# Planning the main slots one early slot sooner, and a pool of their own for the token tiles

## The chip, the core and the metric

The kernel runs on one core of a Trainium2 chip. The metric is the device time of one execution in microseconds. Before the change three runs had a median of 809.41 us (807.67 to 811.24).

## What is computed

A linear attention whose output goes through a mixture of experts with one expert per token. There are 8 batches, 8 heads, 576 positions per batch and head size 64, so 4608 tokens of width 512, and 8 experts with an inner width of 1024. All data are float32.

```python
proj = x @ w_phi                                   # x is q or k, 64 -> 128
proj = proj - max(abs(proj), axis=-1)              # the "differences"
phi  = concatenate([exp(proj), exp(-proj)])
num, den = phi(q) @ (phi(k).T @ v), phi(q) @ sum(phi(k))
x = num / (den + 1e-6)                             # heads side by side: 512 wide
logits = x @ w_gate                                # 8 experts
# the expert of a token: the best one, or that of the token before it (a second gate)
h   = maximum(x @ w1[e], 0)
out = softmax(logits)[e] * (h @ w2[e])
```

Which tokens go to which expert is known only at run time, after the attention. The kernel therefore plans on the chip: it writes lists of tokens per expert to DRAM, works out slots from the counts, reads the lists back and gathers the rows of x.

## The kernel before

**Attention.** `run` goes over 144 chunks of 128 tokens in pairs (`step`). For a pair it projects q and k (`proj`, L210), takes the largest absolute value `m` and subtracts it (L213, L215; the result `sb` holds the differences), takes exponentials for k (`kp`), turns q's differences and takes theirs (`qtr`, L230, L233; `qp`, eight buffers in the pool `feat`), adds up k's features with v (`kv`, L252) and multiplies q's features with that sum (`num`, L311, with results in `xo`, which SyncE writes to DRAM). The right side of the on-chip memory holds, from the outer edge inwards, the pools `front2` (inputs kq and v, 20,128 bytes per partition), `front3` (m, sb, kp, 28,768 bytes) and `feat` (32,768 bytes). On the left lie the constants, the early weights, `moe_xg` (raw weights and gathered tokens), `back2` and `small` (the list buffer `lr` among it).

**Gates.** After every quarter of the tokens `gate` finds each token's expert and its place in that expert's list, counts tokens per expert (`cnt`), and writes list entries by nine scatters of GpSimd (L554). The last gate runs while the first early slot is already being computed; `soon` is a list of eight functions called between the matmul groups of that slot's layer 1, and the last of them (`rest`) finishes the gate with its scatters.

**Slots.** A slot is a run of tokens of one expert. A unit is 128 tokens. There are three early slots of two units each (here called e0, e1, e2), planned during the attention from the gates of the first two and three quarters, and after them the main slots: 3 of four units, 7 of two units, and single and half units. For the main slots `plan_main` makes the plan. It is a generator that is advanced by `more`:

- The first call counts units per expert on TensorE (L637, twice), does some 75 small operations on VectorE (L639 to L785) and issues three list reads on GpSimd (L615; two for the halves, one for all other slots). These must follow all scatters.
- The second call turns the list on TensorE (L628) and copies token numbers and probabilities (`p_tokm`, `p_probm`, L629 and L630).

**A slot's work** (`slots`). `tokens` turns the gathered tokens on TensorE (L903) and splits each into a high and a low part (`xhi` by ScalarE L912, `xlo` by VectorE L913). `layer1` has four groups of 24 matmuls with results in one of two PSUM buffers, from which ScalarE makes `hh` (L952) and VectorE `hl` (L953). `layer2` has 24 matmuls per unit; VectorE scales the result into `y` (L1004) and GpSimd scatters it to the output (L1007). For the early slots layer 2 has one PSUM buffer (`psm4`), later there are two more (`psr`). Every matrix product is three matmuls of high and low parts (L917 to L919).

**Weights.** A slot needs eight tiles of weights, four for each layer. SyncE loads each as 512 KB into a raw buffer (`load`, L840), ScalarE casts it to `whi` (L850), VectorE makes `wlo` (L851). A slot's first load is preceded by reading its expert's number into a register (L827). There are 8 pairs of buffers for weights on the left from the start, 4 on the right from `open_main` on, and one more from `open_rest` on; raw buffers are 3 in `moe_xg` and, from `open_rest` on, 3 more in `moe_l1`, which lies where `back2` and `small` were. The main slots' loads come in program order behind all three early slots.

**Order.** Inside a block a scheduler orders each engine's instructions ahead of time, by their place in the program and by when it expects them to be ready. On the chip each engine then follows that order, each instruction waiting for what it needs. `here` and `issue_after` tie an instruction behind another on the same engine.

Where the calls of `more` stand before: `slots` is called for the early slots with `asides={1: more}` and `final=more`. So the first call stands behind layer 1 of e1 and before its layer 2; the second stands inside layer 1 of e2, behind its second group.

`open_main` opens the right weight pool and behind it one pool `moe_x2` with all of xhi, xlo, hh, hl, y and yl (38,912 bytes), in the place of `front3` and `feat`.

Of the kernel before, what the change touches and what calls it, by code (L numbers as in the profile page):

```python
# [7 lines left out]
F32R = mybir.dt.float32r  # L8
# [41 lines left out]
class Kernel:  # L50
# [9 lines left out]
    def run(self):  # L60
        nc, tc, A = self.nc, self.tc, self.A
        act, dve = self.act, self.dve
        with ExitStack() as root:
            self.const = self.mkpool(root, "const", 1, "left")
            dram = self.mkpool(root, "dram", 1, "left", DRAM)
            self.xs = dram.tile([NT + 1, DM], F32, name="xs")


            self.lst = dram.tile([E * NT + 128, PLACE], F32, name="lst")
            first = self.const.tile([128, 256], F32, name="first")  # L70
            self.sp.dma_start(first[:, 128:256], A["first"][:, 384:512])
            self.ident, self.w2 = first[:, 0:128], first[:, 128:256]
            self.cnt = self.const.tile([128, E], BF16, name="cnt")
            dve.memset(self.cnt, 0.0)

            warm = self.const.tile([128, E], BF16, name="warm")
            act.activation(warm, self.cnt, AF.Exp)

            self.wgi = self.const.tile([128, NHP, 2, 9], F32, name="wgi")
            self.pool.memset(self.wgi, 0.0)  # L80

            self.vs = [[self.const.tile([128, 2, D + 1], F32, name=f"vs{k}{b}") for b in (0, 1)] for k in (0, 1)]
            for x in self.vs:
                for t in x:
                    self.pool.memset(t, 0.0)

            self.moe_early = self.mkpool(root, "moe_e", WE, "left")
            self.mxg = self.mkpool(root, "moe_xg", 2, "left")
            back, front = ExitStack(), ExitStack()
            self.back2 = self.mkpool(back, "back2", 2, "left")  # L90
            self.small = self.mkpool(back, "small", 1, "left")

            self.pr = self.small.tile([128, 2, NC, PLACE], F32, name="pr")
            self.pool.memset(self.pr, 0.0)
            self.pskv = self.mkpool(back, "pskv", 1, "left", PSUM)
            self.psb = self.mkpool(back, "psb", 2, "left", PSUM)


            self.front2 = self.mkpool(front, "front2", 2, "right")
            self.front3 = self.mkpool(front, "front3", 3, "right")  # L100
            self.feat = self.mkpool(front, "feat", 8, "right")
            self.psf = self.mkpool(front, "psf", 2, "right", PSUM)
            self.wphases = [(self.moe_early, WE)]

            self.scattering = False
            self.tail, self.eslots, self.scattered = False, [], []
            self.g, self.ch, self.kvb, self.lg = {}, {}, {}, {}
            n = NBP * NHP * NC
            self.todo, self.turns, self.gates, self.background = [], [], [], []
            self.fetched = 0  # L110
            for gi in range(3):
                self.fetch_kqv(gi)
                if gi == 0:
                    self.sp.dma_start(first[:, 0:128], A["first"][:, 256:384])
                    self.consts()
            with tc.manual_schedule(engines={mybir.EngineType.PE}):
                for p in range(n // 2):
                    while self.fetched < n // 3 and self.fetched * 3 < 2 * p + 8:
                        self.fetch_kqv(self.fetched)
                    if FILL <= p < FILL + 4:  # L120
                        self.fill(p - FILL)
                    self.step(p, n)
            self.tail = True
            p = n // 2
            while p < n // 2 + KVLAG + 1 or self.todo or self.turns or self.gates:
                self.step(p, n)
                p += 1
            for x in self.background:
                for _ in x:
                    pass  # L130
            front.close()
            self.open_main(root)
            plan = self.plan_main()
            more = lambda: next(plan, None)
            go = self.advance

            def rest():
                for _ in self.last_gate:
                    pass
            no = lambda: None  # L140
            self.slots(self.eslots, {1: more}, more, soon=[no, self.fetched_last, go, no, go, no, go, rest])
            back.close()
            self.open_rest(root)
            self.moe()
# [503 lines left out]
    def plan_early(self, bp):  # L648
# [39 lines left out]
        if bp == 1:  # L688
            yield from self.early_chores(slots, got())
        else:  # L690

            g = got()
            for x in g:
                if not self.scattering:
                    break
                yield x

            def last():
                for _ in g:
                    pass  # L700
                for s in slots:
                    self.gather_x(s)

            def soon():
                with self.tc.high_priority():
                    last()
            self.fetched_last = soon
# [95 lines left out]

    def open_main(self, root):
        self.w_right = self.mkpool(root, "moe_wr", WR, "right")
        self.mx2 = self.mkpool(root, "moe_x2", 2, "right")
        self.psm4 = self.mkpool(root, "moe_ps1", 1, "right", PSUM)
        self.psl = self.mkpool(root, "moe_ps2", 2, "right", PSUM)
        self.wphases = [(self.moe_early, WE), (self.w_right, WR)]
# [80 lines left out]
    def tokens(self, s, g, late=False):  # L890

        pe, act, dve = self.pe, self.act, self.dve
        if "xg" not in s:
            self.gather_x(s)

        def step(k, u):
            if k == 0:
                s.setdefault("x", []).append([self.mx2.tile([128, 4, 256], F32R, name=n) for n in ("xhi", "xlo")])
            hi, lo = s["x"][g]
            t = self.turned()  # L900
            with self.here() if late else nullcontext():
                for d in range(4):
                    pe.transpose(t[:, d, :], s["xg"][u][:, d * 128:d * 128 + 128], self.ident)  # L903
            self.parts(s, hi, lo, slice(k * 128, k * 128 + 128), t)
        return [lambda k=k: step(k, sum(s["n"][:g]) + k) for k in range(s["n"][g])]
# [107 lines left out]
            else:  # L1013
                held.append(put)

    def slots(self, order, asides={}, final=None, held=None, soon=()):
        first = order[0]
        for g in range(len(first["n"])):
            for f in self.tokens(first, g):
                f()  # L1020
        self.held = len(first.get("w", ()))
        self.coming = list(order)
        for i, s in enumerate(order):
            while len(s.get("w", ())) < 8:
                self.spare()
            new = order[i + 1] if i + 1 < len(order) else None
            last = len(s["n"]) - 1
            for gi in range(last):
                self.layer1(s, gi, [])
            between = self.tokens(new, 0, bool(soon) and i == 0) if new else [lambda: None, final] if final else []  # L1030
            rest = self.layer1(s, last, between, () if i else soon)
            if i in asides:
                asides[i]()
            for f in between:
                f()
            for gi in range(last + 1):
                self.layer2(s, gi, rest, None if new else held)
            if new and len(new["n"]) == 2:
                for f in self.tokens(new, 1):
                    f()  # L1040
            s.clear()

    def guarded(self, slots, count, i, per):
        if i < len(slots):
            with self.tc.If(count > per * i):
                self.slots([slots[i]])
                self.guarded(slots, count, i + 1, per)
# [103 lines left out]
```

## Time and profile before

| what | value |
|---|---|
| median of 3 runs | 809.41 us |
| the profiled execution | 808.84 us |
| its span, first to last instruction | 807.1 us |
| mean granted clock of TensorE | 0.993 |
| DMA moved | 151.33 MB, mean 188 GB/s |
| weight loads `wraw` | 136 of 512 KB, median 5.0 to 6.0 us to landing |
| weight casts L850 on ScalarE | 136, 1048 ns each |
| weight splits L851 on VectorE | 128, 1222 ns each |
| gathers `xg` for the main slots | 32, median 6.7 us to landing |

Times in the profile are in microseconds from the first instruction. In a timeline a row gives the start, the duration, the engine, the line of the kernel, the operation, what it writes and reads, the number of merged instructions, and in brackets how long the engine had been idle and who released it. PE is TensorE, DVE VectorE, ACT ScalarE, POOL GpSimd, SP SyncE; a small q after the name stands for the engine's sequencer or DMA queue. In the table of waits stand the waiting engine with its tile and line, the awaited one, and the total, the number and the longest of these waits. Matmul durations overlap, so a long row of matmuls takes less time than their sum.

### The profile page before, as it was taken

How to read it: one execution, taken by the hardware profiler on the slowest of the kernel's cores; microseconds unless marked ns; L12 is line 12 of the kernel's file. 1: busy time of each engine (PE TensorE's matmuls, PEld its weight loads, DVE VectorE, ACT ScalarE, POOL GpSimd, SP SyncE). 2: the span in 40 equal slices, each digit the busy share in tenths (PEclk: the TensorE clock that was granted, in tenths of full speed). 3: DMA queues.
4: the chain of work that ended last, by engine and by line, in shares of the span. 5: the costliest groups of instructions: out<-in, count | busy, mean ns of one | idle time of the engine just before them, and what ended most of it. 6: DMA issues, size and time to landing. Idle time of an engine off the chain costs nothing.

```text
span 807.1 us, 23180 instructions
## 1 busy us (share of the span) xinstructions
PE 772.1 (96%) x9674; PEld 679.6 (84%) x9674; DVE 513.5 (64%) x940; ACT 401.1 (50%) x708; POOL 156.1 (19%) x165
## 2 busy tenths in 40 slices
PE   6899999999999998999799999999999999999993
PEld 5899989998898887987698997698988988589883
DVE  5687798789878886766653224643866823768621
ACT  4666666666587565351542123532745713657410
POOL 0000001200275241153411102201421311110100
PEclk9999999999999999999999999999999999999998
DMA  6754445444677714451952775832966769959300
GB/s 197 220 150 130 135 129 143 131 135 128 184 233 226 211 52 126 141 186 48 385 186 90 269 276 209 288 97 97 362 200 203 265 236 411 349 193 319 117 27 15
DMA packets 77231, 151.33 MB, mean 188 GB/s; under 512 B 8524, under 2 KB 50828, under 8 KB 77078
## 3 DMA queue, kind: packets, MB, share of 16 engines
q1 hardware_dynamic: 67424, 127.33, 47.9%
q0 software_dynamic: 7424, 20.08, 7.0%
q10 hardware_dynamic: 2272, 2.37, 0.9%
q8 instruction: 78, 1.28, 0.6%
q14 instruction: 33, 0.27, 0.1%
HBM read 128.21 MB, written 22.06 MB: 186 GB/s over the span
## 4 chain that ended last, share of the span: by engine, by line
PE 64%; issue 15%; DMA 8%; DVE 7%; POOL 2%; ACT 2%; SPq 1%; POOLq 0%; DVEq 0%; ACTq 0%
PE l L917 10%; PE l L918 10%; PE l L919 10%; PE kvp L252 8%; PE pj L210 8%; PE nm L311 8%; PE qt L230 4%; DMA out<-y,p_tokm 4%; DMA wraw<-in_w2h 2%; PE l L930 2%; POOL out L1007 1%; DVE m L213 1%; DVE sb L215 1%; PE nm L290 1%; PE tr L903 1%
## 5 line engine op out<-in xcount | busy, mean ns | idle before, releaser
L850 ACT CAST whi<-wraw 128x1024 fp32r<-128x1024 f32 x136 | 142.1, 1048 | 153.8 <-PE l L919 68.2
L851 DVE TENSOR_TENSOR wlo<-wraw,whi 128x1024 fp32r<-128x1024 f32 x128 | 156.0, 1222 | 77.4 <-ACT whi L850 76.4
L917 PE MATMUL l<-xhi,whi 128*128 128x256 f32 x512 | 146.9, 287 | 1.3 <-ACT xhi L912 1.3
L918 PE MATMUL l<-xlo,whi 128*128 128x256 f32 x512 | 144.6, 282 | 1.3 <-DVE xlo L913 1.3
L919 PE MATMUL l<-xhi,wlo 128*128 128x256 f32 x512 | 144.7, 283 | 0.0
L917 PE MATMUL l<-whi,hh 128*128 128x512 f32 x288 | 115.0, 399 | 5.5 <-DVE y L1004 5.4
L213 DVE TENSOR_REDUCE m<-pj 128x8 f32<-128x1024 f32 x72 | 87.8, 1219 | 44.7 <-PE pj L210 43.4
L919 PE MATMUL l<-whi,hl 128*128 128x512 f32 x288 | 114.0, 396 | 1.0 <-DVE hl L953 1.0
L918 PE MATMUL l<-wlo,hh 128*128 128x512 f32 x288 | 114.1, 396 | 0.0
L233 ACT ACTIVATE qp<-qt 128x512 f32<-128x512 f32 x144 | 84.6, 604 | 53.5 <-PE qt L230 53.1
L219 ACT ACTIVATE kp<-sb 128x512 f32<-128x512 f32 x144 | 82.8, 622 | 51.1 <-DVE sb L215 43.4
L917 PEld LDWEIGHTS l<-xhi,whi 128*128 128x128 f32 x512 | 97.0, 190 | 3.5 <-issue 2.2
L918 PEld LDWEIGHTS l<-xlo,whi 128*128 128x128 f32 x512 | 97.1, 190 | 1.8 <-DVE xlo L913 1.5
L919 PEld LDWEIGHTS l<-xhi,wlo 128*128 128x128 f32 x512 | 97.0, 190 | 0.1
L210 PE MATMUL pj<-first,kq 64*128 64x128 f32 x1152 | 86.4, 291 | 6.2 <-DMA kq<-in_kqT 6.2
L215 DVE TENSOR_TENSOR sb<-pj,m 128x1024 f32<-128x1024 f32 x72 | 88.1, 1224 | 4.1
L311 PE MATMUL nm<-kvs,qp 128*64 128x74 f32 x2304 | 86.3, 228 | 1.0 <-ACT kvs L292 1.0
L1007 POOL DMA_INDIRECT out<-y,p_tokm x31 | 39.2, 1265 | 245.9 <-DVE y L1004 245.3
L210 PEld LDWEIGHTS pj<-first,kq 64*128 64x128 f32 x1152 | 72.3, 193 | 11.8 <-issue 4.9
L311 PEld LDWEIGHTS nm<-kvs,qp 128*64 128x64 f32 x2304 | 79.0, 136 | 1.8 <-ACT kvs L292 1.5
L252 PE MATMUL kvp<-v,kp 128*64 128x65 f32 x2048 | 76.2, 224 | 0.0
L952 ACT ACTIVATE hh<-l 128x512 fp32r<-128x512 f32 x64 | 38.0, 594 | 75.6 <-PE l L919 75.6
(230 smaller groups left out, 1057.1 us busy)
## 6 DMA issues: line engine op xcount, KB each, us to landing
wraw<-in_w1h SPq DMA_DIRECT2D x68, 512.0 KB, 6.0
wraw<-in_w2h SPq DMA_DIRECT2D x68, 512.0 KB, 5.0
kq<-in_kqT SPq DMA_DIRECT2D x47, 384.0 KB, 4.0
v<-in_va SPq DMA_DIRECT2D x48, 195.0 KB, 4.3
xs<-xo SPq DMA_DIRECT2D x48, 128.0 KB, 2.5
whi<-in_w1h SPq DMA_DIRECT2D x8, 512.0 KB
wlo<-in_w1h SPq DMA_DIRECT2D x8, 512.0 KB, 5.3
whi<-in_w2h SPq DMA_DIRECT2D x8, 512.0 KB
```

Of the source, the lines that this page charges most:

```text
L210: self.last_pe = self.pe.matmul(t[:, h, i % 2, j, :], kq[r, j, s], self.w2[r], start=True, stop=True)
L213: dve.tensor_reduce(m, f, AX.X, ALU.max, apply_absolute_value=True)
L215: self.last_dve = dve.tensor_sub(sb.rearrange("p h c j f -> p (h c j) f"), f, m.unsqueeze(2).broadcast_to([128, 8, 128]))
L219: self.last_act = act.activation(kp[:, :, :, sg, :].rearrange("p c h f -> p h c f"), sb[:, :, :, 0], AF.Exp, scale=1.0 - 2 * sg)
L233: self.act.activation(qp[:, sg], t, AF.Exp, scale=1.0 - 2 * sg)
L252: self.pe.matmul(self.kvp[r, sg, h], self.ch[i]["kp"][:, h, sg, r], self.v(i, b)[:, h], start=first and n < 2, stop=last and n >= 6)
L311: self.pe.matmul(e["t"][r, c - c0, h, :], self.ch[i]["qp"][:, sg, h, q0 + r.start:q0 + r.stop], kvs[:, sg, h, :], start=sg == 0, stop=sg == 1)
L850: self.act.copy(hi, raw)
L851: (low or self.dve).tensor_sub(lo, raw, hi.bitcast(F32))
L917: mm(o, ah, bh, start=first, stop=False)
L918: mm(o, ah, bl, start=False, stop=False)
L919: self.last_pe = mm(o, al, bh, start=False, stop=last)
```

## The change

`slots` takes a further list, `later`. In the first early slot it becomes the list of functions that layer 2 calls: behind its first and third group of matmuls in the first unit, and behind the first in the second unit. The first two do nothing, the third is `more`. So the first call of the plan stands in e0's layer 2, behind the first three matmuls of its second unit. The calls in e1 (`asides`) and in e2 (`final`) stay; they are now the second and the third. The third finds the generator at its end.

`open_main` opens a pool `moe_x2` for xhi and xlo alone (two buffers of each, 16,384 bytes) right behind the right weight pool, and behind that a pool `moe_h2` for hh, hl, y and yl.

```diff
-            self.slots(self.eslots, {1: more}, more, soon=[no, self.fetched_last, go, no, go, no, go, rest])
+            self.slots(self.eslots, {1: more}, more, soon=[no, self.fetched_last, go, no, go, no, go, rest],
+                       later=[no, no, more])
...
         self.w_right = self.mkpool(root, "moe_wr", WR, "right")
-        self.mx2 = self.mkpool(root, "moe_x2", 2, "right")
+
+        self.mxt = self.mkpool(root, "moe_x2", 2, "right")
+        self.mx2 = self.mkpool(root, "moe_h2", 2, "right")
...
-                s.setdefault("x", []).append([self.mx2.tile([128, 4, 256], F32R, name=n) for n in ("xhi", "xlo")])
+                s.setdefault("x", []).append([self.mxt.tile([128, 4, 256], F32R, name=n) for n in ("xhi", "xlo")])
...
-    def slots(self, order, asides={}, final=None, held=None, soon=()):
+    def slots(self, order, asides={}, final=None, held=None, soon=(), later=()):
...
             rest = self.layer1(s, last, between, () if i else soon)
+            if soon and i == 0:
+                rest = later
             if i in asides:
                 asides[i]()
```

## The prediction

> **What bounds the kernel now.** I read the head of the page first, then the table by stage, the waits of TensorE, the timeline around its longest wait, and the chain of waits there.
>
> ```profile
> span 807.1 us, 23180 instructions
> PE 772.1 (96%) x9674; PEld 679.6 (84%) x9674; DVE 513.5 (64%) x940; ACT 401.1 (50%) x708; POOL 156.1 (19%) x165
> ```
>
> TensorE is busy for 772.1 of 807.1 us. A change that removes no matmul can win only from the 35 us in which it stands still, and from stretches at a lower clock. The table by stage says where those are near this change. Its columns are the stretch, its length, the busy time and count of each engine, the granted clock, the DMA share and GB/s.
>
> ```profile
> 312.00:324.00 12.00, 8.23 (x174) 7.27 (x170) 9.58 (x29) 5.39 (x10) 0.00 (x0) 1.00 0.64 193
> 366.00:378.00 12.00, 10.34 (x58) 8.79 (x58) 8.92 (x71) 0.30 (x1) 4.80 (x5) 1.00 0.16 49
> 378.00:392.00 14.00, 13.64 (x92) 11.95 (x90) 5.13 (x8) 4.92 (x7) 6.51 (x6) 1.00 0.69 254
> 392.00:412.00 20.00, 15.55 (x90) 13.58 (x91) 15.40 (x18) 12.71 (x16) 6.89 (x6) 0.91 0.97 373
> 412.00:436.00 24.00, 24.00 (x181) 22.95 (x181) 11.38 (x14) 7.98 (x12) 1.92 (x2) 1.00 0.29 102
> ```
>
> Three holes: 312 to 324 (the change from the attention part to the first early slot, e0), 366 to 378 (inside the second early slot, e1), and 392 to 412 (from the third, e2, to the first main slot), the only one with a clock below 1.00. From 412 on TensorE has no hole, so what is won before it arrives at the end undiminished. The waits of TensorE from 310 to 430 name the causes (waiter, awaited, us in total, times, longest):
>
> ```profile
> PE l L917 <- DVE y L1004: 5.4, 2, 4.1
> PE l L917 <- ACT xhi L912: 1.3, 1, 1.3
> PE l L918 <- DVE xlo L913: 1.3, 1, 1.3
> PE l L919 <- DVE hl L953: 1.0, 2, 0.6
> ```
>
> Both waits on `y` are the same event. Layer 2 of an early slot has one PSUM buffer (`psm4`), so its second unit starts only when VectorE has scaled the first unit's result out of it. The timeline of TensorE and of VectorE at the two places:
>
> ```profile
> 369.93 0.50 PE L917 MATMUL l<-whi,hh 128*128 128x512 f32 x1 [1.31 <-DVE y L1004]
> 393.38 1.47 PE L903 MATMUL tr<-first,xg 128*128 128x128 f32 x12
> 398.96 0.50 PE L917 MATMUL l<-whi,hh 128*128 128x512 f32 x1 [4.11 <-DVE y L1004]
> ```
>
> ```profile
> 342.63 0.75 DVE L1004 TENSOR_SCALAR y<-l,p_probe 128x512 f32<-128x512 f32 x1 [2.32 <-PE l L919]
> 346.21 1.23 DVE L851 TENSOR_TENSOR wlo<-wraw,whi 128x1024 fp32r<-128x1024 f32 x1 [2.83 <-ACT whi L850]
> 363.97 0.22 DVE L639 TENSOR_SCALAR p_um<-pt 36x8 int32<-36x8 f32 x2
> 364.59 1.21 DVE L851 TENSOR_TENSOR wlo<-wraw,whi 128x1024 fp32r<-128x1024 f32 x1
> 369.13 0.73 DVE L1004 TENSOR_SCALAR y<-l,p_probe 128x512 f32<-128x512 f32 x1
> 374.47 0.14 DVE L604 TENSOR_SCALAR p_rim<-p_rowm 36x1 int32<-36x1 f32 x1
> 397.02 1.23 DVE L851 TENSOR_TENSOR wlo<-wraw,whi 128x1024 fp32r<-128x1024 f32 x1 [1.08 <-ACT whi L850]
> 398.16 0.74 DVE L1004 TENSOR_SCALAR y<-l,p_probf 128x512 f32<-128x512 f32 x1
> ```
>
> In e1 the `y` at 369.13 stands among the plan's small operations (363.97 to 374.47). In e2 it stands behind a weight split, which waited for a cast, which waited for a load. The chain of waits shows that load:
>
> ```profile
> 384.60 0.57 DVE hl L953
> 385.17 12.01 DMA wraw<-in_w2h
> ...
> 398.16 0.75 DVE y L1004
> 398.96 0.50 PE l L917
> ```
>
> A weight load of the first main slot, issued at 385.17, held the chain for 12.01 us, in a stretch with the DMA engines 0.97 busy. So e2 pays for the first main slot's weights coming late. Why they come late is in SyncE's timeline and in the rows of line 827 (registers read from the plan):
>
> ```profile
> 350.26 7.45 SPq L840 DMA_DIRECT2D wraw<-in_w2h  x4
> 382.33 2.06 SPq L840 DMA_DIRECT2D wraw<-in_w1h  x4
> ```
>
> ```profile
> L827 SPq TENSOR_LOAD <-p_eim x14: 267/274/529, 373.6 to 381.3; - x14
> ```
>
> The last early load goes out by 357.7. Then SyncE sends nothing until 382.33: it waits for the plan, reads 14 expert numbers (373.6 to 381.3, about 0.6 us each with their checks), and only then loads.
>
> **The change, part by part.** *The plan.* `more` is called three times. Its first call issues the TensorE counts (L637), some 75 VectorE operations and the three list reads of POOL (L615); the second issues the turning of the list (L628), the numbers and the probabilities. Both move one step ahead: the first from behind e1's layer 1 to behind the first three matmuls of e0's second unit, the second from e2's layer 1 to behind e1's layer 1. The third finds nothing left and costs nothing. No instruction is added.
>
> ```profile
> 361.05 0.21 PE L637 MATMUL pt<-cnt,consts 128*36 128x8 bf16 x2
> 380.44 0.41 PE L628 MATMUL pt<-first,lr 40*128 40x40 f32 x2
> ```
>
> ```profile
> 351.37 0.96 POOL L554 DMA_INDIRECT lst<-pr,ri  x1 [0.30 <-issue]
> 354.51 2.03 POOL L1007 DMA_INDIRECT out<-y,p_toke  x1 [0.30 <-issue]
> 374.93 0.92 POOL L615 DMA_INDIRECT lr<-lst,p_rim  x1 [2.31 <-DVE p_rim L604]
> ```
>
> New times, worked out from these. e0's first unit ends at about 342.6 (its `y`), eight filling matmuls of e1's layer 1 follow (24.00 us for 181 matmuls in 412 to 436, 0.13 us each, so 1.1), then three of the second unit at twice that, so the counts run at about 344.5 instead of 361.05. Before, the last plan operation came 374.47 - 361.05 = 13.4 us later, with other VectorE work between; so the row numbers are ready at 357.9 if that stays so (354 if the queue is emptier). The list must be written before it is read: the last scatter leaves POOL at 352.3, so this does not end later than the plan. The list read leaves 0.5 us later (374.93 - 374.47), at about 358.4, and lands by the row below within 4.5 us: 362.9.
>
> ```profile
> DMA to landing us min/median/max: 2.6/3.4/4.5
> ```
>
> The turning stands in TensorE's order where L637 stood, at 361.05. Behind it are e1's layer 2 and everything else, so TensorE would wait 0 to 1.9 us for the list; I take 0.7. On SyncE the expert numbers are ready at about 355 to 357 and their reading takes 8 us: 363 to 366. Three of the main slots' six raw buffers lie in the memory that the back pools give free, the list's buffer among it, so the loads also wait for the turning, about 362 to 363. The first main load goes at about 365 instead of 382.33, 17 us earlier. The burst that filled 392 to 412 then falls into 366 to 378, where DMA was 0.16 busy; e2's own loads are through by then. All its weights are split by about 383, before the fillers ahead of e2's second unit (393.38).
>
> What this removes: the 4.11 us before 398.96, since nothing late stands ahead of e2's `y` any more; and the slow clock after it. The stage has 0.91, and 9% of 20 us is 1.8 us. The 1.31 us before 369.93 also goes, since the plan has left that place; at e0, with the same eight filling matmuls and an empty VectorE queue, the row at 342.63 was followed by no wait.
>
> The slow clock followed the 4.11 us of idleness and not the 1.31 us (1.00 in 366 to 378). So a remainder of up to 1.3 us costs nothing extra, and one between 1.3 and 4.1 costs between 0 and 1.8 us. The Trainium skill, "TensorE: Matmul & The Clock Gate", Part 1, sets the border at one idle window of about 3.4 us; by that a remainder of 3 us would still keep the 1.8 us in the sum, and by the nearest row (4.11) it might lose them. No row here lies between.
>
> What the plan costs in its new place: VectorE's plan (363.97 to 374.61 less a split of 1.21, an `hl` of 0.6 and a `y` of 0.73, so 8.1 us) fall into e0's second unit and e1's layer 1. There they delay splits for e2, which e2 needs only from about 368, and e0's second `y`, whose PSUM buffer is wanted again at 361. Without that slack each would cost TensorE its delay, up to 1.6 us as at 369.13. The burst moved to 366 to 378 puts waiting splits ahead of e2's `hl`; the same has cost 0.6 and 0.4 us before (the row of L953, 1.0 in all), so I take 0.5 more, between 0 and 2.
>
> *The pool.* The token tiles (xhi, xlo, 16,384 bytes) get their own pool next to the right weight pool; hidden tiles and results follow. The sum and the stretch of memory stay the same. What can change is what the first token tile waits for:
>
> ```profile
> 320.13 1.07 ACT L912 CAST xhi<-tr 128x512 fp32r<-128x512 f32 x2 [2.94 <-PE nm L311]
> 321.30 0.48 PE L917 MATMUL l<-xhi,whi 128*128 128x256 f32 x2 [1.27 <-ACT xhi L912]
> 323.05 0.38 PE L918 MATMUL l<-xlo,whi 128*128 128x256 f32 x1 [1.27 <-DVE xlo L913]
> ```
>
> The casts wait for the last matmul that reads the features, at 320.03 (321.30 - 1.27). If the new pool lay over the differences alone, they could run before that, and the two waits of 1.27 us, 2.5 us, would go. But the bytes don't fit: weight pool 32,768 + token pool 16,384 = 49,152, against 20,128 (inputs) + 28,768 (differences and key features) = 48,896. The pool reaches 256 bytes into the query features' pool. In the compiled kernel before, the first cast into the right weight pool waits for an instruction that only reads a neighbour tile which it does not cover (`m`), so a new pool waits for the whole of every pool it touches. I take 0, with 2.5 us as the other end.
>
> **The sum.** Against the profiled execution (808.84 us, span 807.1): 4.1 + 1.8 + 1.3 - 0.7 - 0.5 = 6.0 us, giving 802.8. That execution lay 0.6 under the median of 809.41, so the forecast is 803.4.
>
> **The rivals.** *The tokens start early too.* The waits are drawn by tile or bytes and the 256 bytes don't matter, or their buffer is free in time. 6.0 + 2.5: 800.9. Against it stands the wait on `m`. Chance 0.12.
>
> *The stall moves instead of going.* Loads from 365 on land while e1's first `y` is due (368, since TensorE stood from 368.62). If splits of late loads stand ahead of a `y` again, 4.1 + 1.8 come back: 809.3. For it: the same order of VectorE's queue produced the wait at 398.96. Against it: by 368 the first load is only 3 us old, and all are through when e2's `y` is due. Chance 0.20.
>
> *The plan moves but the loads do not*, because something else holds the first main load (the reading of numbers put behind other work, or raw buffers). Then only the 1.3 us at e1 goes: 808.1. Chance 0.08.
>
> *Slower: TensorE waits for the list.* If the plan's operations are queued behind e2's splits, the last of which ended at 365.8 (364.59 + 1.21), the list read leaves at about 366.4 and lands 4.5 us later, at 371, and TensorE stands before the turning from 361 for 10 us, with the slow clock 11.8 us. Against the 7.2 us of removed waits that is 4.6 us slower: 814.0. It decides from a landing at about 366.5. For it: such splits lie on VectorE from 346.21 on. Against it: the plan stands ahead of them in the program. Chance 0.08.
>
> **How the numbers follow.** The forecast has 0.52, with its own range from 801.2 (nothing lost, and the 1.0 us of `hl` waits gone too) to 806.5 (1.9 for the list, 2 for `hl`, and 0.4 more). 0.5% of the median, about what a measurement of this kernel can tell from no change, is 4.05 us: faster means under 805.4. From the forecast 0.45 lies there, with 0.12 of the first rival 0.57. No change: 0.07 of the forecast, 0.20, 0.08, and 0.03 of the last: 0.38. Slower: 0.05. The range goes from 800.0 to 809.6; it takes in the stall that moves and leaves out the last rival.
>
> **What would show it.** Right: L637 at about 344, the last L615 before 360, L628 at 361 to 363, the first main load of L840 at 363 to 366; no wait over 1 us on `y`; clock 1.00 in e2's second unit; the e0 rows of 1.27 unchanged. Wrong in a step: a wait before L628 of over 2 us; a wait on `y` or `hl` over 2 us between 365 and 395; the xhi casts before the last `nm`. It would be wrong as a whole if the first main load stayed after 375.

## The result and the profile after

| | before | after |
|---|---|---|
| median of 15 runs each | 810.14 us (807.67 to 813.39) | 806.13 us (804.18 to 808.9) |
| ratio to before, 95% interval | | 0.9946 (0.9934 to 0.9957) |
| the profiled execution | 808.84 us | 804.8 us |
| its span | 807.1 us | 803.0 us |

The change makes the kernel 4.4 us faster by the ratio (0.54%). The forecast was 803.4 us, 6.0 us under its base; the median lies inside the range. Lines behind the first edit have moved by one, those below L804 by three: in the profile after, `y` is L1007, `hl` L956, `xhi` and `xlo` are L915 and L916, the weight casts and splits L853 and L854, the loads L843, the counts L638, the list read L616, the turning L629.

The head of the page after, with engines, busy time and share:

```profile
span 803.0 us, 23183 instructions
PE 771.9 (96%) x9674; PEld 678.7 (85%) x9674; DVE 512.5 (64%) x940; ACT 401.4 (50%) x708; POOL 156.3 (19%) x165
```

The work is the same; what changed is where TensorE stands still and at which clock it runs. The table by stage of after (stretch, length, busy us and count of PE, PEld, DVE, ACT, POOL, granted clock, DMA share, GB/s):

```profile
312.00:324.00 12.00, 8.22 (x194) 7.26 (x191) 9.01 (x27) 5.29 (x10) 0.00 (x0) 1.00 0.68 200
366.00:378.00 12.00, 11.55 (x60) 9.15 (x60) 3.75 (x8) 0.62 (x2) 4.81 (x5) 1.00 0.38 112
378.00:392.00 14.00, 13.48 (x91) 11.90 (x90) 8.65 (x9) 8.45 (x11) 5.53 (x5) 1.00 1.03 402
392.00:412.00 20.00, 18.48 (x127) 16.55 (x126) 14.54 (x18) 10.81 (x14) 6.73 (x6) 1.00 0.74 271
412.00:436.00 24.00, 24.00 (x164) 22.17 (x163) 9.36 (x12) 6.79 (x10) 2.93 (x3) 1.00 0.23 78
```

The hole at 312 to 324 is as deep as before (8.22 against 8.23 us busy). 366 to 378 has won 1.2 us of busy time, 392 to 412 has won 2.9 and the full clock. The weight traffic that filled 392 to 412 now fills 378 to 392: not 366 to 378, where the prediction put it. The waits of TensorE from 300 to 430 in after:

```profile
PE l L921 <- DVE xlo L916: 1.3, 1, 1.3
PE l L920 <- ACT xhi L915: 1.3, 1, 1.3
PE l L920 <- DVE y L1007: 0.9, 1, 0.9
PE l L922 <- DVE hl L956: 0.6, 1, 0.6
```

The two waits at e0 stand as they were. On `y` 0.9 us is left of 5.4. Why it is not zero is in VectorE's timeline of after:

```profile
345.38 0.23 DVE L640 TENSOR_SCALAR p_um<-pt 36x8 int32<-36x8 f32 x2 [1.16 <-PE pt L638]
...
347.39 1.23 DVE L854 TENSOR_TENSOR wlo<-wraw,whi 128x1024 fp32r<-128x1024 f32 x1
...
367.97 0.13 DVE L605 TENSOR_SCALAR p_rim<-p_rowm 36x1 int32<-36x1 f32 x1
...
392.93 2.37 DVE L854 TENSOR_TENSOR wlo<-wraw,whi 128x1024 fp32r<-128x1024 f32 x2
395.21 0.74 DVE L1007 TENSOR_SCALAR y<-l,p_probf 128x512 f32<-128x512 f32 x1
```

The plan starts at 345.38, about where the prediction had it, and its last needed result, the row numbers, comes at 367.97 instead of 357.9. One row of the table by stage for the splits L854 alone (VectorE's busy us and count come first, then POOL's) says what lies between:

```profile
345.38:368.10 22.72, 10.96 (x9) 0.00 (x0) 1.00 0.54 167
```

Nine weight splits, 10.96 us (the last one for e1 and all eight for e2), stand among the plan's operations; in the old place it was one. The list read (GpSimd), the turning (TensorE) and the first main loads (SyncE) follow from that, one fence each:

```profile
368.42 0.92 POOL L616 DMA_INDIRECT lr<-lst,p_rim  x1 [6.29 <-DVE p_rim L605]
```

```profile
373.60 0.41 PE L629 MATMUL pt<-first,lr 40*128 40x40 f32 x2
```

```profile
374.14 2.05 SPq L843 DMA_DIRECT2D wraw<-in_w1h  x4
```

The loads start at 374.14: 8.2 us earlier than before and not 17. TensorE did not wait at the turning, because in its order the turning now stands inside e1's second unit of layer 2 and not at the end of e1's layer 1. And the chain of waits of after at e2's `y` has the same shape as before:

```profile
382.15 10.81 DMA wraw<-in_w2h
392.99 1.06 ACT whi L853
...
394.14 1.08 issue
395.21 0.76 DVE y L1007
```

A late load, its cast, its split, `y`. Only the end comes earlier relative to TensorE.

What the change is worth in its own stage is read from e0's first turning of tokens to that of the second main slot, first in before, then in after:

```profile
314.10 1.09 PE L903 MATMUL tr<-first,xg 128*128 128x128 f32 x8
452.29 1.03 PE L903 MATMUL tr<-first,xg 128*128 128x128 f32 x8
```

```profile
314.89 1.09 PE L906 MATMUL tr<-first,xg 128*128 128x128 f32 x8
448.30 1.03 PE L906 MATMUL tr<-first,xg 128*128 128x128 f32 x8
```

138.19 us became 133.41: 4.8 us, in one execution of each. In the table by stage over these two stretches, again first before and then after, the length less TensorE's busy time gives its idle time, 10.34 and 6.30 us:

```profile
314.10:452.29 138.19, 127.85 (x881) 113.17 (x880) 80.81 (x198) 49.01 (x66) 38.02 (x35) 0.99 0.50 174
314.89:448.30 133.41, 127.11 (x881) 111.78 (x880) 79.58 (x198) 49.18 (x66) 38.23 (x35) 1.00 0.53 180
```

The span shows 0.8 less, since this execution came to e0 0.8 us later. There the kernels don't differ; the granted clock became full at 14.1 us in the one and at 15.8 in the other, and from 14 to 16 us 45 matmuls began in before and 34 in after.

### The profile page after: what moved, and what is told of

Same layout as the page of the kernel before. It is cut to its first block, busy times and chain, and to the rows that moved or that the text cites. A ratio compares the mean times of both kernels' runs of the same rounds, so it can differ in the third digit from the quotient of the medians.

```text
span 803.0 us, 23183 instructions
## 1 busy us (share of the span) xinstructions
PE 771.9 (96%) x9674; PEld 678.7 (85%) x9674; DVE 512.5 (64%) x940; ACT 401.4 (50%) x708; POOL 156.3 (19%) x165
## 3 DMA queue, kind: packets, MB, share of 16 engines
q8 instruction: 78, 1.28, 0.7%
## 4 chain that ended last, share of the span: by engine, by line
PE 63%; issue 15%; DMA 8%; DVE 7%; POOL 3%; ACT 2%; SPq 1%; POOLq 0%; DVEq 0%; ACTq 0%
PE l L920 9%; PE l L921 9%; PE l L922 9%; PE kvp L253 9%; PE pj L211 8%; PE nm L312 8%; PE qt L231 4%; DMA out<-y,p_tokm 4%; DMA wraw<-in_w2h 3%; PE l L933 2%; POOL out L1010 2%; DVE m L214 1%; DVE sb L216 1%; PE tr L906 1%; PE nm L291 1%
## 5 line engine op out<-in xcount | busy, mean ns | idle before, releaser
L853 ACT CAST whi<-wraw 128x1024 fp32r<-128x1024 f32 x136 | 142.2, 1048 | 164.0 <-PE l L922 68.0
L854 DVE TENSOR_TENSOR wlo<-wraw,whi 128x1024 fp32r<-128x1024 f32 x128 | 156.2, 1223 | 71.7 <-ACT whi L853 70.4
L956 DVE SCALAR_TENSOR_TENSOR hl<-l,hh 128x512 fp32r<-128x512 f32 x64 | 43.9, 686 | 44.2 <-ACT hh L955 44.2
```

The source lines that it names most:

```text
L853: self.act.copy(hi, raw)
L854: (low or self.dve).tensor_sub(lo, raw, hi.bitcast(F32))
```

## The experiments

The theory after the comparison: the gain comes from e2 (the wait on `y` and the half clock behind it) and from e1; it is smaller than forecast because the plan, placed among e2's splits, releases the main loads late; and the pool gives nothing, for want of 256 bytes. The rivals: the pool has a part in the gain; the loads' time doesn't matter, only that VectorE is rid of the plan; the stall only moves. Each run stands against the kernel before on the same chip.

**The two halves of the change alone.** First the pools alone:

```diff
+        self.mxt = self.mkpool(root, "moe_x2", 2, "right")
+        self.mx2 = self.mkpool(root, "moe_h2", 2, "right")
...
```

> Only the pool is split; the plan's calls stay where they were. My theory: the token pool reaches 256 bytes into the features' pool, and a new pool waits for the whole of every pool it touches, so the two 1.27 us waits on xhi and xlo at the first early slot stay and the time is that of before, ratio 1.000 (0.997 to 1.003). Rival, the split gives part of the 4.4 us gained: the two waits go, 2.5 us less, ratio 0.997, and the xhi casts come before the last nm matmul.

Measured: 810.7 against 810.2 us, ratio 1.0001 (0.9989 to 1.0012). The waits at e0 are there, 1.28 and 1.27. Then the plan alone, with the pool `moe_x2` left whole:

```diff
-            self.slots(self.eslots, {1: more}, more, soon=[...])
+            self.slots(self.eslots, {1: more}, more, soon=[...], later=[no, no, more])
...
```

> Only the plan's call moves; the pool stays one. My theory: all of the gain is here, ratio 0.9945 (0.993 to 0.996), the wait on y in the third early slot falls from 4.1 to about 0.9 us, the one in the second is gone, and no stretch at half clock follows. Rival, the split gives part: ratio 0.9975 with these waits unchanged from the changed kernel's, or with larger ones.

Measured: 806.0 us, ratio 0.9943 (0.992 to 0.9965), with waits of 0.65 and 0.88 at e2, as in after. So all of the change's gain is the plan's, and the pool's part is nothing within the interval, which leaves about 0.9 us either way.

**The 256 bytes.** The change with a tile of 256 bytes per partition added to `front3` and set to zero, so that the token pool ends where `feat` begins:

```diff
             self.front3 = self.mkpool(front, "front3", 3, "right")
+            pad = self.front3.tile([128, 64], F32, name="pad", bufs=1)
+            self.pool.memset(pad, 0.0)
```

> The changed kernel with one more tile of 256 bytes in front3, so that the token pool lies over front3 alone. My theory: the xhi casts no longer wait for the last nm matmul, the two 1.27 us waits go, 2.5 us less than the changed kernel, ratio to before 0.9915 (0.990 to 0.993). Rival, the casts wait for something else as well (ScalarE's and VectorE's queues are full there): the waits stay and the ratio is 0.9945.

Measured: 801.9 against 810.2 us, ratio 0.989 (0.987 to 0.9911). The stage of e0, and ScalarE's casts there:

```profile
312.00:324.00 12.00, 10.89 (x212) 9.94 (x207) 9.03 (x26) 5.33 (x10) 0.00 (x0) 1.00 0.66 190
```

```profile
316.18 0.60 ACT L917 CAST xhi<-tr 128x512 fp32r<-128x512 f32 x1
316.98 0.59 ACT L917 CAST xhi<-tr 128x512 fp32r<-128x512 f32 x1
```

The casts run over 4 us earlier (320.93 in after), before the last matmul on the features, and TensorE is busy for 2.7 us more of the 12. The gain is a little above the range expected (ratio 0.990 to 0.993). The same two edits without the plan:

> The kernel before with the pool split alone and 256 bytes more in the differences' pool, the plan where it was. Theory A (the split gives nothing in the change because the token pool reaches 256 bytes into the query features' pool and a new pool waits for the whole of each pool that it touches): the casts of e0's token tiles run before the last nm, the two waits of 1.27 us at e0 go, and the kernel is 2.0 to 3.0 us faster than before, ratio 0.9963 to 0.9975; the waits of 1.3 at e1 and of about 4 to 5 at e2 stay. Rival (the padded kernel won through an earlier plan, not at e0, or e0's gain comes back as a longer wait at e2, since the loads' times stay): ratio 0.998 to 1.000 with e2's wait longer by what e0 won.

Measured: 806.8 against 811.2 us, ratio 0.9958 (0.9943 to 0.9974), with e0's waits gone and e2's at 4.75 us. The prediction's reason for taking the pool at 0 is right: the token pool reached 256 bytes into a pool that it did not need, and waited for all of it. It is worth rather more than the 2.5 us of the two waits. In the profiled executions the stage from e0's first turning of tokens to that of the second main slot took 134.74 us (314.45 to 449.19) against 138.19: 2.7 us less idle at e0, and the 1.0 us of waits on `hl` is gone too, while the wait on `y` at e2 grew by 0.6. The rest is taken up below, with the clock.

**Is it the splits ahead of `y`?** In the kernel before, the splits of the first main slot from the fourth on are placed behind e2's first `y`:

```diff
+        with self.tc.issue_after(self.last_y.ins) if first and len(s["w"]) >= 3 else nullcontext():
             (low or self.dve).tensor_sub(lo, raw, hi.bitcast(F32))
...
```

> The kernel before, with the plan where it was, but the fourth and later weight splits of the first main slot are put behind the third early slot's first y on VectorE. Theory A, the 4.1 us were an order in VectorE's queue (y behind splits whose loads were late): the wait and the half clock go, 5 to 6 us less, ratio 0.993 to 0.995, although the first main load still goes out at 382. Theory B, the weights themselves are late and the wait only moves to the first main slot's layer 1: TensorE then waits there for a split, 2 to 5 us between 395 and 415, ratio 0.998 to 1.000.

Measured: 810.0 us, ratio 0.9999 (0.9982 to 1.0016). TensorE's timeline:

```profile
394.74 0.50 PE L919 MATMUL l<-whi,hh 128*128 128x512 f32 x1 [0.92 <-DVE y L1006]
...
411.18 0.58 PE L919 MATMUL l<-xhi,whi 128*128 128x256 f32 x1 [4.06 <-DVE hl L955]
```

The wait on `y` falls from 4.11 to 0.92 us, and one of 4.06 us appears in the first main slot's layer 1. There `hl` waits for `hh`, which stands on ScalarE behind the cast of a later load (408.85, cast L850). This is the stall that moves: this change of VectorE's order is worth nothing while the weights come late.

**The plan early, the loads late.** In the kernel with the plan alone, a small copy behind e2's last `hl` reads a tile of the pool that the later raw buffers lie over, which holds back the main loads:

```diff
+            def late():
+                with tc.issue_after(self.last_hl.ins):
+                    dve.tensor_copy(self.const.tile([128, 1], F32, name="late"), self.pr[:, 0, 0, 0:1])
-            self.slots(self.eslots, {1: more}, more, soon=[...], later=[no, no, more])
+            self.slots(self.eslots, {1: more}, late, soon=[...], later=[no, no, more])
...
```

> The change's plan without the pool split, but the second half of the plan's step ahead is taken back: a small copy on VectorE behind e2's last hl holds the release of the list's buffers, so that the first main load goes at about 382 again while the row numbers are ready at about 368 as with the change. Theory A (the gain comes from the main loads leaving SyncE earlier, and the plan only matters through them): the 1.3 us at e1 are won, the wait of 4 us on e2's y and the half clock behind it come back; ratio to the kernel before 0.997 to 1.000, first main load at 380 to 384, a wait of 3.5 to 5 us near 396 to 399, clock 0.85 to 0.93 in that stage. Rival (the gain comes from VectorE having the plan behind it when e2's splits and y are due): the wait on y stays under 1.5 us although the loads are late; ratio 0.993 to 0.996.

Measured: 807.5 against 811.2 us, ratio 0.9956 (0.994 to 0.9973). The first main load goes at 382.13. TensorE and VectorE at e2, and the table by stage there:

```profile
395.30 0.50 PE L922 MATMUL l<-whi,hh 128*128 128x512 f32 x1 [2.21 <-DVE y L1009]
```

```profile
390.80 3.79 DVE L856 TENSOR_TENSOR wlo<-wraw,whi 128x1024 fp32r<-128x1024 f32 x3 [0.38 <-ACT whi L855]
394.50 0.74 DVE L1009 TENSOR_SCALAR y<-l,p_probf 128x512 f32<-128x512 f32 x1
```

```profile
392.00:396.00 4.00, 1.79 (x14) 1.47 (x12) 3.89 (x5) 3.54 (x7) 2.90 (x3) 1.00 1.00 392
396.00:400.00 4.00, 4.00 (x13) 3.13 (x12) 4.00 (x6) 2.90 (x4) 2.24 (x2) 0.57 0.95 339
```

Neither theory as written. With the loads as late as before, the wait still fell from 4.11 to 2.21: VectorE's order now has four splits ahead of this `y` where the kernel before had five; the half clock stayed. The earlier loads bring the rest: 2.21 to 0.88 and the clock. From e0's first turning of tokens to that of the second main slot, the 138.19 us of before became 134.89 here (314.11 to 449.00) and 132.85 with the plan alone (315.10 to 447.95). So by the traces, one execution each, 3.3 us of the gain come without an earlier load (1.3 at e1 and 1.9 on this `y`) and 2.0 with it. By time alone this run can't be told from the plan's half of the change; the split of the gain is the trace's. No run changed the order alone in this way, so that the order is what took the 1.9 us is argued, not shown.

**An earlier plan.** The padded kernel with the plan's first call one place further ahead, at the end of e0's layer 1, and its second at the end of e1's:

```diff
             def rest():
                 for _ in self.last_gate:
                     pass
+                more()
...
```

> The padded kernel with the first step of the plan one place earlier again, at the end of e0's layer 1, and the second at the end of e1's. Theory A (what is left of the prediction's sum, waits of 0.9 on e2's y and 1.3 on hl, is there because the plan's 75 operations are spread among e2's splits and end at 368 instead of 358): the plan now stands mostly in a row ahead of those splits, the row numbers are ready by 358 to 360, the list lands by 364, the first main load leaves at 364 to 368, the waits of 1.3 and 0.9 fall to under 0.5 each; ratio to the kernel before 0.986 to 0.988, against 0.989 of the padded kernel. Rival 1 (the loads leave earlier but the remaining waits come from the order of VectorE's queue, splits ahead of hl and y, whenever the loads land): ratio as padded, 0.988 to 0.990, with waits of 0.5 to 1.3 at other places. Rival 2 (the plan in e0's layer 1 delays e0's y and hl): new waits of 1 us or more between 335 and 350; ratio 0.990 to 0.993.

Measured: 805.2 against 811.2 us, ratio 0.9936 (0.992 to 0.9952): slower than the padded kernel, and for a reason that none of the three expectations names. TensorE, GpSimd and the table by stage:

```profile
366.04 0.44 PE L632 MATMUL pt<-first,lr 40*128 40x40 f32 x2 [6.58 <-DMA lr<-lst,p_rim]
```

```profile
349.81 0.95 POOL L558 DMA_INDIRECT lst<-pr,ri  x1 [0.30 <-issue]
...
355.95 0.91 POOL L619 DMA_INDIRECT lr<-lst,p_rih  x1 [3.88 <-issue]
...
360.99 0.92 POOL L619 DMA_INDIRECT lr<-lst,p_rim  x1 [0.31 <-issue]
```

```profile
364.00:371.00 7.00, 4.96 (x13) 3.92 (x14) 3.17 (x5) 0.89 (x1) 3.40 (x3) 0.51 0.50 174
```

This is the prediction's slower rival, TensorE waiting for the list, made real: 6.58 us at the turning and 6.8 us at half clock. The row numbers no longer hold the list: they are there at 351.98. GpSimd does: its last scatter leaves at 349.81, the first list read at 355.95, and the one for the main slots stands behind two others and an output at 360.99, 9 us after its row numbers. The loads leave at 366.61, and from there to 412 no wait above 0.3 us is left.

Next, the same kernel with each slot's reading of its expert numbers on SyncE tied behind the last load of the slot before it:

> The kernel with the plan at the end of e0's layer 1, and each slot's expert numbers read by SyncE only behind the last load of the slot before it, instead of all 14 ahead of the first main load (about 8 us). If that reading is what holds the first main load once the list is early: the first main load leaves 3 to 7 us earlier than in that kernel, at 360 to 364, and the ratio to the kernel before falls by 0.001 to 0.002. Rival (the list's landing and its turning on TensorE hold it, and the reading lies beside that wait): first main load within 1.5 us of that kernel's, same ratio within 0.001.

Measured: ratio 0.9941 (0.9924 to 0.9958), first main load 366.66. The run decides nothing, since the edit moved no reading: in the kernel with the early plan only five of the 14 stood ahead of the first main load, and five do here. The rows of these readings, first of that kernel, then of this one:

```profile
L833 SPq TENSOR_LOAD <-p_eim x5: 268/272/278, 350.3 to 358.4; - x5
L834 SPq TENSOR_LOAD <-p_eim x5: 266/272/281, 350.2 to 358.7; - x5
```

The first row answers the question without the edit. The reading was through about 8 us before the load, and the load left 0.57 us after the turning of the list (366.04 to 366.61). So the list decides, and the reading lies beside that wait.

Last, the same early first call with the turning moved into e1's second unit of layer 2:

```diff
-            self.slots(self.eslots, {1: more}, more, soon=[...], later=[])
+            self.slots(self.eslots, {}, None, soon=[...], later=[no, no, more])
...
-            if soon and i == 0:
+            if soon and i == 1:
                 rest = later
```

> The plan's first step stays at the end of e0's layer 1, but the turning of the list, which made TensorE wait 6.6 us there, is moved into the second unit of e1's layer 2, about 8 us later. Theory (the early plan lost only by that wait and its slow clock; the loads then leave as soon as the list is turned): no wait at the turning, which comes at about 368; first main load 367 to 370, 1 to 4 us before that of the padded kernel; the waits of 1.3 on hl and 0.9 on y of the padded kernel fall to under 0.5 each; 0.5 to 2 us faster than the padded kernel beside it. Rival (the remaining waits come from how splits, hl and y stand in VectorE's queue, whenever the loads land): within 0.5 us of the padded kernel, with a wait of about 1 us somewhere from 375 to 400.

Measured: 800.05 us (798.83 to 800.24) against 810.14, ratio 0.9868 (0.9848 to 0.9888). Beside it on the same chip the padded kernel once more:

> The padded kernel once more, beside the last one: ratio to the kernel before 0.987 to 0.991 as in its first measurement.

Measured: 801.6 us (800.64 to 802.95), ratio 0.9894 (0.9876 to 0.9912). The single times don't overlap, the intervals do a little. The turning comes at 366.37 without a wait, the first main load at 366.91. TensorE's and VectorE's timelines:

```profile
377.60 0.39 PE L923 MATMUL l<-xhi,whi 128*128 128x256 f32 x1 [0.76 <-DVE hl L959]
388.55 0.50 PE L925 MATMUL l<-whi,hl 128*128 128x512 f32 x1 [0.59 <-DVE hl L959]
391.16 0.50 PE L923 MATMUL l<-whi,hh 128*128 128x512 f32 x1 [0.54 <-DVE y L1010]
```

```profile
385.40 2.50 DVE L857 TENSOR_TENSOR wlo<-wraw,whi 128x1024 fp32r<-128x1024 f32 x2 [0.26 <-ACT whi L856]
...
389.21 1.23 DVE L857 TENSOR_TENSOR wlo<-wraw,whi 128x1024 fp32r<-128x1024 f32 x1 [0.72 <-ACT whi L856]
390.36 0.75 DVE L1010 TENSOR_SCALAR y<-l,p_probf 128x512 f32<-128x512 f32 x1
```

The loads' part of the theory holds, the waits' part doesn't: from 375 to 395 they fall from 2.2 us in the padded kernel beside it (0.63, 0.56, 1.06) to 1.9, not to under 0.5 each. Ahead of `y` stands now the ninth split, of the second main slot. In these kernels, loads that leave earlier have more splits ahead of the same `y`:

| kernel | first main load | splits ahead of e2's first `y` | last of them ends | wait on `y` | half clock behind it |
|---|---|---|---|---|---|
| before | 382.33 | 5 | 398.25 | 4.11 | yes |
| held back | 382.13 | 4 | 394.59 | 2.21 | yes |
| after | 374.14 | 8 | 395.30 | 0.88 | no |
| padded | 371.14 | 8 | 392.30 | 0.87 | no |
| two steps | 366.91 | 9 | 390.44 | 0.54 | no |

## Why the prediction was right, and where it was wrong

*The mechanism was right in its main line.* e2 paid for the first main slot's weights coming late, and an earlier plan let them go earlier. The wait on e2's `y` was taken at 4.1 us and 3.2 came (4.11 to 0.88); the half clock at 1.8 and 1.7 came (1.00 after); e1's wait at 1.3 and all of it came: no wait on `y` is left there. The plan alone gives all of it. But the prediction put the whole wait on `y` down to the loads. With the loads held back 1.9 of the 3.2 us went all the same, and the earlier loads brought 1.3 and the clock. The run with the tied splits shows only that another order on VectorE, with late loads, gains nothing.

*The step that failed* is "before, the last plan operation came 13.4 us later, with other VectorE work between; so the row numbers are ready at 357.9 if that stays so". It didn't stay so: 22.8 us passed from the counts (345.17) to the row numbers (367.97), since nine splits of 10.96 us lie there, where the old place, counted in the same way, had two (at 362.83 and 364.59). The prediction had seen these splits, in its slower rival, and had argued that the plan stands ahead of them in the program; place in the program didn't decide. From this one term follow the list read at 368.42 instead of 358.4 and the first main load at 374.14 instead of 365. Of the signs that it named for being right, the last list read, the turning (373.60 instead of 361 to 363) and the first main load failed, and the load came 0.9 us ahead of the 375 after which it would have called itself wrong as a whole. That the time still lies in the range is partly luck: less of the gain hung on the loads than it thought.

*The size of the gain.* It also wrote that all the first slot's weights are split by about 383, 18 us after the first load; measured were 21.2 us (374.14 to 395.30), and with the loads at 366.91 still 21 us (to 387.9, where the two splits at 385.40 end). With about the forecast's load time the waits from 375 to 395 are still 1.9 us, as many as in after (0.25, 0.64, 0.88 and 0.18). So the end of the waits at e2, taken as complete, was the mis-sized term: 0.88 us on `y` was left in after, and 0.54 in the kernel whose loads leave at 366.91, beside two waits on `hl`.

*Waits that didn't come.* The 0.7 us at the turning were zero, because its place in TensorE's order moved too. For `hl` it took 0.5 us more, and 0.5 came: in after one wait of 0.64 us stands in the place of the 0.6 and 0.4, and four of 0.18 to 0.25 us are new (on `hl` and `hh`, and one put down to `p_rim`).

*The sum.* 3.2 + 1.7 + 1.3 = 6.2, less the 0.5 us of short waits: 5.7. The stage won 4.8. The waits are all there, since TensorE's idle time fell by 4.0 us (10.34 to 6.30); but its busy time fell by only 0.7 us, where the end of the half clock alone gives 1.7. So about 1 us came back in busy time, which the prediction has no term for; what it is was not traced. The span shows 4.1, through the start; the median 4.0 and the ratio 4.4.

*The rivals.* "The tokens start early too" did not happen, for the reason given, and one tile of 256 bytes makes it happen. "The stall moves" was tried by itself and gives no gain. "The plan moves but the loads do not" was priced at the 1.3 us of e1 and measured at 3.6 (ratio 0.9956): when the plan moves, what stands ahead of `y` changes too. "TensorE waits for the list" met its condition in after, a list that lands past 366.5, but not its price, since the turning had moved behind it; the kernel with the plan at the end of e0's layer 1 paid 6.58 us and the clock.

## The clock

That the half clock follows an idleness between 1.3 and 4.1 us was left open in the prediction. The held-back kernel has it after 2.21 us: in 396 to 400 the mean clock of 0.57 means 3.4 us at half speed (0.43 x 4 / 0.5). And the kernel with the pools alone has it behind e0:

```profile
320.00:324.00 4.00, 1.45 (x13) 1.19 (x10) 3.90 (x16) 1.34 (x3) 0.00 (x0) 1.00 0.83 268
324.00:328.00 4.00, 4.00 (x21) 3.77 (x20) 0.66 (x7) 0.55 (x1) 0.00 (x0) 0.57 0.05 16
```

Two waits of 1.28 and 1.27 us with half a microsecond of matmuls between them were followed by 3.4 us at half clock in this execution and in that with the tied splits, and by none in the profiled executions of before, after, the plan alone and the held-back loads, which have the same waits. All half-clock pieces between 300 and 420 in these traces are 3.4 or 6.8 us long.

The traces show what decides. The changes of the granted clock lie whole multiples of 3.413 us apart: in before the record begins at full clock at 14.13, and the half clock at 399.83 comes 113 times 3.413 us later. Cut each execution into stretches of 3.413 us on this grid. From 310 to 420, in all 12 profiled executions, a stretch at full clock with up to 1.76 us of idle TensorE was followed by full clock, and one with 1.84 us or more by half clock. The two nearest to this border, with the stretch that follows each, first the plan alone and then the tied splits:

```profile
319.86:323.27 3.41, 1.65 (x40) 1.32 (x34) 3.00 (x10) 1.07 (x2) 0.00 (x0) 1.00 1.01 339
323.27:326.69 3.42, 2.63 (x22) 2.63 (x23) 2.27 (x13) 0.26 (x1) 0.00 (x0) 1.00 0.29 86
```

```profile
320.53:323.94 3.41, 1.57 (x11) 1.40 (x12) 3.38 (x14) 0.73 (x2) 0.00 (x0) 1.00 0.74 232
323.94:327.36 3.42, 3.42 (x18) 3.20 (x17) 0.41 (x4) 0.29 (x1) 0.00 (x0) 0.50 0.00 0
```

With the pools alone 1.99 us of the two waits fall into one stretch; in before 1.27 us fall into each of two. So it is where the grid lies that tells these kernels apart at e0. (The profile models the ends of matmuls, so the border is rough.)

The Trainium skill, "TensorE: Matmul & The Clock Gate", Part 1, describes a monitor window of 3413 ns that runs freely, so that the time of a change depends on where in it the first matmul lands. The lengths, the grid and the chance at e0 agree with that. The Trainium skill, in the same part of that page, puts the border for half clock at one idle window of about 3.4 us. That does not agree: an idleness of 2.21 us was enough here, and so were two shorter ones.

One piece of 3.4 us at half clock costs 1.7 us, 0.002 of the time. The padded kernel's 11 runs have a mean clock of 0.993 to 0.995, the 15 of after 0.985 to 0.995, with 4.4 us between their ratios where the removed waits are 2.5. In the profiled executions, neither of which has half clock there, the stage differs by 2.8 us (133.41 and 130.65). That the rest is the clock behind e0 fits, but was only argued: the runs without a profile don't say where their clock was low.

## What to carry to other kernels

When a block of small operations is moved, its new duration is what lies among it in the new place, not its old one: count the work that becomes ready there. A load that leaves earlier ends a wait only if what stands ahead of the waiting instruction in its engine's queue doesn't grow with it; look at which split it stands behind, not at when the first one is through. And a new pool's bytes should be counted against the pools that it replaces: 256 bytes too many cost 2.5 us of waits here, more than half of what the whole change gained.

## What was not expected of the hardware

Granted half clock after an idleness of 2.21 us, and after two of 1.3 us in some executions, by how much of one stretch of the grid was idle (above). The list's way takes long by itself: with the plan at the end of e0's layer 1, 6.1 us passed from GpSimd's last scatter (349.81) to the first list read (355.95) though that read's row numbers were there, and in no run was the list turned before 366. What fills the 6.1 us was not traced.
